# A Fourier-mixing layer and one routed feed-forward token on one core: fewer and longer VectorE operations

## The chip, the core and the metric

One core of a Trainium2 chip runs the whole kernel in one launch. The metric is the device time in microseconds. Each time shown is one execution; the kernel before was run three times, and one more execution was profiled. Where the text says TensorE, VectorE, ScalarE, GpSimd and SP, the profile says PE (and PEld for its weight loads), DVE, ACT, POOL and SP.

## The reference, cut to what matters

With S = 2048 tokens, D = 576 and F = 4608, all float32:

```
h  = x + Re(DFT_seq(DFT_hid(layernorm(x))))   # four matrices given as inputs
z  = layernorm(h)
r  = z @ w_r                                  # one score per token
t  = argmax(r)                                # one token is routed
y  = (silu(z[t] @ w_gate) * (z[t] @ w_up)) @ w_down * sigmoid(r[t])
out = h + z, and y is added to row t
```

## The kernel before

**Data.** x lies in SBUF as X[128, 16, 576], 16 slots of 128 tokens. The sequence matrices (`ct`) are read in blocks of 128 x 9 x 128 float32, 576 KB each. The kernel computes with folded halves of them and of the hidden matrix (`wt`), and it also checks on the chip that the matrices have the symmetry that this folding needs: VectorE forms differences (`off_s`, `off_t`, `off_h`, `off_w`), ScalarE squares and sums them. If the sum is not small, a slower general path runs behind a branch; with these inputs it doesn't. The three weights of the feed-forward part (`wg`, `wu`, `wd`, each 128 x 36 x 576) follow in 27 loads of 1152 KB.

**Stages.** (1) X arrives in nine loads. For each slot, `fold_d` (L454) writes the sum of a row's two mirrored halves and, in a second operation (L466), their difference; `measure` (ScalarE) takes the variance; `from_mean` (L493), `scales` and `diag` (L528) follow for a row group. `X_RUNS` are the five row groups. `diag` writes ident times the slot's 1/sd, a 128 x 128 matrix that TensorE multiplies the folded rows with (`fold`), so that they are scaled on the way. GpSimd does the row groups' small products (`ends`, `totals`, `biases`), whose last line L521 writes the offset column of the folded rows XF. (2) `seq` multiplies XF by the sequence blocks, in two groups of five steps, `hid` by the hidden matrix, and `residual` adds the result to X. Behind it, per slot, ScalarE takes the variance of h and VectorE its product with w_r (`dot_h`, L623). In three batches `scores` (L635 to L644) computes 1/sd, the scores R, and the two factors UP and BB with which ScalarE (`result`, L661) or GpSimd (slots 0 and 8) turns h into the output rows in X; these are stored. (3) `argmax` finds the token, `where`, `row_of_token` (L1039) and `to_all` bring its normalized row to all partitions; `copy_xs` (L1084) writes it to SBUF as xs. (4) The feed-forward part runs in nine blocks of four columns of weights. Products with xs go to VectorE, or to GpSimd with the sums on ScalarE; `gated` (L1225 to L1228) then forms H for four columns with one ScalarE and two VectorE operations, and `down` (L1236) multiplies H by `wd` on TensorE into one row, which `last_of_row` (L1249) adds up and `last_store` writes out.

The dot product subtracts the mean like this: `copy_wr` (ScalarE) spreads w_r over the partitions and keeps its sum; `scores` then computes (h . w_r) - mean(h) sum(w_r) with L639 and multiplies it by 1/sd with L640.

**Order.** Nothing is scheduled by hand. `Plan` takes operations with an engine, a cost in microseconds and what they wait for, and orders each engine's queue by list scheduling; the order is fixed when the program is built. Each queue runs in order, so an operation that waits holds up what is behind it on its engine. SP's queue carries the direct loads and the late stores, GpSimd's queue the mirrored loads (gathers, L301) and the early stores between its arithmetic. A load into a buffer waits for the last reader of what was there. In the feed-forward part there are 16 buffers, so the first 16 loads are issued early and the other eleven each wait for a buffer; `plan_ffn` plans six times and keeps the plan that ends first:

```
for b in range(NJ // TW):
    j = TW * b
    for w in "gu":
        for r in (0, JW):
            products_of(w, j + r)
    gate_and_down(j, j + TW)
    load_to(N_BUF + 3 * (b + 1))
```

`store_if` (L1060) stores slots 4 to 8 and 0 (1440 and 288 KB) under a condition, at one of two places in SP's queue: ahead of the last loads if the token is among those slots, behind them if not.

## Time and profile before

| | us |
|---|---|
| three runs | 199.27, 200.22, 200.1 (median 200.1) |
| the profiled execution | 199.06 |
| its span, first to last instruction | 197.1 |
| busy: PE, DVE, ACT, POOL | 130.2, 166.4, 140.5, 111.8 |
[...]
| moved by DMA | 77.81 MB, mean 395 GB/s |

The busy shares are averages over stages with different limits. An operation's time runs from its start until its result is written, and the next one on the engine can start a little earlier, so sums of busy times come out slightly too large. Idle time of an engine matters only where it delays what ends last.

### The profile page before, as it was taken

What the parts mean: (1) busy time and instruction counts of PE and PEld (TensorE: products, weight loads), DVE (VectorE), ACT (ScalarE), POOL (GpSimd) and SP (SyncE); (2) the same over time, 40 slices, a digit from 0 to 9 for tenths busy, and PEclk for the clock granted to TensorE, in tenths of its full rate; (3) what the DMA queues carried; (4) which work ended last, traced back from release to release, by engine and by line L of the source; (5) the groups of instructions that cost most, each with busy time, mean ns of one, the idle gap of its engine ahead of it and who ended that gap; (6) DMA issues with size and microseconds to landing.
All of it is one profiled execution on the core that took longest, in us unless ns stands there. A gap on an engine that the chain in (4) does not pass through costs nothing. (4 is left out here: it accounts for less than half of the span.)

```text
span 197.1 us, 2789 instructions
## 1 busy us (share of the span) xinstructions
PE 130.2 (66%) x758; PEld 89.5 (45%) x758; DVE 166.4 (84%) x419; ACT 140.5 (71%) x259; POOL 111.8 (57%) x134
## 2 busy tenths in 40 slices
PE   0007889999999999999999986700241317074940
PEld 0004667755667788676866764400121103032330
DVE  4399999989899699995999999999839999987620
ACT  3298865781997879797588599989527999787600
POOL 6588888724447882398830000004556999999700
PEclk9999999999999999999999999985555555567596
DMA  5999999999999999999999999999999999999980
GB/s 183 422 412 413 409 415 406 411 394 326 401 406 396 406 379 410 409 406 415 407 408 416 422 425 419 428 421 409 430 429 417 432 423 425 423 424 421 419 354 24
DMA packets 14491, 77.81 MB, mean 395 GB/s; under 512 B 1855, under 2 KB 1859, under 8 KB 11143
## 3 DMA queue, kind: packets, MB, share of 16 engines
q1 hardware_dynamic: 10461, 56.56, 71.1%
q0 software_dynamic: 4000, 21.03, 26.5%
q8 instruction: 7, 0.11, 0.2%
q14 instruction: 13, 0.11, 0.1%
q10 hardware_dynamic: 10, 0.00, 0.0%
HBM read 72.86 MB, written 6.49 MB: 403 GB/s over the span
## 5 line engine op out<-in xcount | busy, mean ns | idle before, releaser
L368 ACT ACTIVATE Q<-Q 128x2944 bf16<-128x2944 bf16 (+5 forms) x26 | 55.4, 2132 | 15.7 <-DVE Q L380 8.2
L610 PE MATMUL py<-W,Z 128*128 128x289 f32 x180 | 45.3, 409 | 2.5 <-DVE X L619 2.5
L565 PE MATMUL ps<-D,XF 128*128 128x320 f32 (+3 forms) x216 | 44.8, 408 | 0.4 <-DMA D<-in_ct_dram 0.4
L610 PEld LDWEIGHTS py<-W,Z 128*128 128x128 f32 x180 | 33.6, 189 | 13.9 <-issue 2.2
L301 POOL DMA_INDIRECT R<-in_ct_dram,ic x21 | 29.3, 1396 | 18.0 <-DVE Q L375 14.1
L565 PEld LDWEIGHTS ps<-D,XF 128*128 128x128 f32 (+1 forms) x216 | 32.1, 172 | 12.8 <-issue 2.4
L1209 POOL TENSOR_TENSOR D<-D,Z 128x1152 f32<-128x1152 f32 x8 | 20.9, 2640 | 0.0
L667 POOL DMA_DIRECT2D out_dram<-X x1 | 0.6, 606 | 33.5 <-ACT X L661 33.5
L301 POOL DMA_INDIRECT D<-in_ct_dram,ic x11 | 14.8, 1346 | 7.6 <-DMA R<-in_ct_dram,ic 4.6
L498 ACT ACTIVATE junk<-X,XT 128x576 bf16<-128x576 f32 x16 | 12.3, 772 | 7.6 <-DVE W L459 6.4
L1214 ACT ACTIVATE junk<-D 128x576 bf16<-128x576 f32 x20 | 13.7, 683 | 3.2 <-POOL D L1209 1.6
L375 DVE TENSOR_TENSOR Q<-R,D 128x896 bf16<-128x896 f32 x11 | 11.9, 1084 | 3.9 <-DMA D<-in_ct_dram 2.4
L1236 PE MATMUL pd<-XF,H 128*1 128x144 f32 x80 | 5.3, 438 | 14.8 <-DVE H L1228 11.3
L537 PE MATMUL fo<-W,diag 128*128 128x288 f32 (+1 forms) x8 | 3.7, 640 | 16.0 <-DVE diag L528 16.0
L380 DVE TENSOR_TENSOR Q<-R,D 128x1152 bf16<-128x1152 f32 x10 | 13.4, 1348 | 0.0
L630 ACT ACTIVATE junk<-X,TD 128x576 bf16<-128x576 f32 x16 | 12.3, 766 | 1.4 <-DVE X L619 1.3
L661 ACT ACTIVATE X<-X,BB,UP 128x576 f32<-128x576 f32 x14 | 10.8, 854 | 3.1 <-DVE BB L642 3.1
L387 DVE TENSOR_TENSOR Q<-D 128x640 bf16<-128x640 f32 (+3 forms) x20 | 12.8, 694 | 0.0
L623 DVE SCALAR_TENSOR_TENSOR junk<-X,wr 128x576 bf16<-128x576 f32 x16 | 12.1, 755 | 0.3
L375 DVE TENSOR_TENSOR Q<-D 128x896 bf16<-128x896 f32 x11 | 11.8, 1082 | 0.0
L619 DVE SCALAR_TENSOR_TENSOR X<-py,X 128x576 f32<-128x576 f32 x16 | 11.6, 748 | 0.0
L375 DVE TENSOR_TENSOR Q<-R 128x896 bf16<-128x896 f32 x10 | 10.7, 1083 | 0.2 <-DMA R<-in_ct_dram,ic 0.2
(202 smaller groups left out, 257.5 us busy)
## 6 DMA issues: line engine op xcount, KB each, us to landing
D<-in_ct_dram SPq DMA_DIRECT2D x22, 576.0 KB
R<-in_ct_dram SPq DMA_DIRECT2D x10, 576.0 KB
D<-in_wu_dram SPq DMA_DIRECT2D x5, 1152.0 KB
D<-in_wd_dram SPq DMA_DIRECT2D x4, 1152.0 KB
R<-in_wg_dram SPq DMA_DIRECT2D x3, 1152.0 KB
D<-in_wg_dram SPq DMA_DIRECT2D x3, 1152.0 KB
out_dram<-X SPq DMA_DIRECT2D x2, 1440.0 KB
X<-in_x_dram SPq DMA_DIRECT2D x4, 576.0 KB
```

What stands on the lines that cost most here:

```text
L301: pool.indirect_dma_start(tile, None, view, bass.IndirectOffsetOnAxis(ap=rows, axis=0), element_offset=at)
L368: act.activation(t, t, AF.Square, accum_out=DS[0 : t.shape[0], n : n + 1])
L375: dve.tensor_tensor(o, C[j, i, True][:, 0:7, :], C[j, i, False][:, 7:0:-1, :], op=SIGN[i])
L380: dve.tensor_tensor(o, C[NK - j, i, False], C[j, i, False][:, :, ::-1], op=SIGN[i])
L387: dve.tensor_tensor(o[:, :, k::2, :], t[:, :, k::2, 0:HM], t[:, :, k::2, HM:P], op=op)
L498: act.activation(junk[:, 0:D], X[:, k, 0:D], AF.Square, bias=XT[:, n : n + 1], scale=-float(D), accum_out=VX[:, n : n + 1],)
L565: pe.matmul(cm(ZP[g, n][k % 2][p0 : p0 + m], w), XF[:, q, m0 : m0 + m], DT[g, i][:, :, k, 0:HM], start=k in (0, 1), stop=k in (6, 7),)
L610: pe.matmul(YP[GROUPS[g][c]][:, h, 0:w], Z[:, a, c * P : (c + 1) * P], w_block(a)[:, h * HD : h * HD + w], start=(a == 0), stop=(a == 4),)
L623: dve.scalar_tensor_tensor(junk2, X[:, k, 0:D], 1.0, wr, op0=OP.mult, op1=OP.mult, accum_out=TD[:, n, 0:1])
L630: act.activation(junk[:, 0:D], X[:, k, 0:D], AF.Square, bias=TD[:, n, 1:2], scale=-float(D), accum_out=VAR[:, n : n + 1],)
L1209: pool.tensor_tensor(t, t, xs.unsqueeze(1).to_broadcast([P, JW, D]), op=OP.mult)
L1214: act.activation(junk[:, 0:D], WB[w, j][:, r, :], AF.Copy, accum_out=acc[:, j + r : j + r + 1])
```

## The change

- `fold_d` is split: `sum_d` for one slot, `diff_d` for one or two slots that came with one load (six pairs and four singles).
- `from_mean` goes from VectorE to GpSimd, as two operations (the factor D first, then the subtraction).
- 14 `diag` become four `diags`, of 2, 4, 4 and 4 slots, as one product of two operands that repeat (ident over the slots, 1/sd over the columns).
- The one-column copy of `off_w` goes to GpSimd as `off_w0`.
- `copy_wr` subtracts the mean from w_r with a third ScalarE operation, so that `scores` needs only a product; UP and BB are made by `factors` on GpSimd, in three operations, and results and QX wait for those.
- `check_sum` does two comparisons in one operation.
- Blocks 0 and 1, 2 and 3, 4 and 5 of the feed-forward part are gated together; the last three stay single.
- The costs given to the planner change with the operations.

```diff
-        dve.tensor_copy(o[:, 575:576], im[:, 0:1])
+    def off_w0(n, u):
+        ps = W_ROWS[n]
+        pool.tensor_copy(Q[0:ps, u % 2, 3 * D - 1 : 3 * D], W["ABC"[n]][0:ps, 1, 0:1])
...
+    def diff_d(k, m):
+        t, a, b = UF[k][:, 289:D], X[:, k : k + m, 1:HD], X[:, k : k + m, D - 1 : HD : -1]
+        step = UF[k + m - 1].offset - UF[k].offset
+        t = bass.AP(tensor=t.tensor, offset=t.offset, ap=[list(t.ap[0]), [step, m], [1, HD - 1]])
         if k > 8:
             a, b = b, a
-        dve.tensor_tensor(t[:, 289:D], a, b, op=OP.subtract)
+        dve.tensor_tensor(t, a, b, op=OP.subtract)
...
-        pool.tensor_tensor(DX2[:, n0:n1], DX[:, n0:n1], DX[:, n0:n1], op=OP.mult)
+        pool.tensor_scalar(DX2[:, n0:n1], DX[:, n0:n1], float(D), None, op0=OP.mult)
+        pool.tensor_tensor(DX2[:, n0:n1], DX2[:, n0:n1], DX[:, n0:n1], op=OP.mult)
...
-        dve.scalar_tensor_tensor(v, DX2[:, n0:n1], -float(D), v, op0=OP.mult, op1=OP.add)
+        pool.tensor_tensor(v, v, DX2[:, n0:n1], op=OP.subtract)
...
-        dve.tensor_scalar(t, ident, RX[:, n : n + 1], None, op0=OP.mult)
+    def diags(n0, n1, u):
+        m = n1 - n0
+        t = DGT[:, u * P : (u + m) * P].rearrange("p (n c) -> p n c", n=m)
+        dve.tensor_tensor(
+            t, ident.unsqueeze(1).to_broadcast([P, m, P]), RX[:, n0:n1].unsqueeze(2).to_broadcast([P, m, P]),
+            op=OP.mult,
+        )
...
-        dve.scalar_tensor_tensor(r, tot, wsum[:, 1:2], dot, op0=OP.mult, op1=OP.add)
-        dve.tensor_mul(r, r, rs)
-        dve.tensor_scalar(cols(UP, js), cols(RS, js), 1.0, None, op0=OP.add)
-        dve.scalar_tensor_tensor(
-            cols(BB, js), tot, -1.0 / D, cols(RS, js), op0=OP.mult, op1=OP.mult
-        )
+        dve.tensor_mul(r, dot, rs)
+
+    def factors(js):
+        tot, rs = cols(TD, js)[:, :, 1], cols(RS, js)
+        pool.tensor_scalar(cols(UP, js), rs, 1.0, None, op0=OP.add)
+        pool.tensor_tensor(cols(BB, js), tot, rs, op=OP.mult)
+        pool.tensor_scalar(cols(BB, js), cols(BB, js), -1.0 / D, None, op0=OP.mult)
...
+        act.activation(halves_of(wr), YP["wr"][:, :, 0:HD], AF.Identity, bias=wsum[:, 1:2])
+    DG_RUNS = [(0, 2), (2, 6), (6, 10), (10, 14)]
...
         f = add("DVE", 1.5, then(scores, js), v, [n for j in js for n in DOT[j]], push=push)
         SCORES.append(f)
+        f = add("POOL", 0.6, then(factors, js), f, push=push + 10.0)
+        FACTORS.append(f)
...
-    qx = add("DVE", 0.4, from_result, SCORES)
+    qx = add("DVE", 0.4, from_result, FACTORS)
...
-            gate_and_down(j, j + TW)
-            load_to(N_BUF + 3 * (b + 1))
+            if b % 2 or b >= 6:
+                gate_and_down(j0, j + TW)
+                j0 = j + TW
+                load_to(N_BUF + 3 * (b + 1))
```

## Rows read from the trace of the kernel before

**Rows 1.** The page's second part: the DMA line of the span in 40 equal slices. A digit is the mean busy share of the core's 16 DMA engines in tenths.

```profile
DMA  5999999999999999999999999999999999999980
```

**Rows 2.** The stage table: busy time in six stretches of the span. Columns: the stretch and its length in us, busy us (and instructions) of PE, PEld, DVE, ACT and POOL, the granted TensorE clock, the DMA share and the GB/s moved.

```profile
10.00:30.00 20.00, 12.84 (x45) 9.20 (x46) 18.88 (x88) 16.58 (x42) 16.98 (x52) 1.00 1.02 411
30.00:105.00 75.00, 74.34 (x337) 54.35 (x336) 68.88 (x104) 55.81 (x72) 44.97 (x36) 1.00 1.02 399
105.00:130.00 25.00, 19.36 (x78) 14.05 (x76) 24.80 (x55) 20.40 (x35) 0.00 (x0) 1.00 1.01 422
130.00:153.40 23.40, 4.08 (x10) 2.60 (x10) 18.83 (x74) 16.38 (x27) 11.44 (x19) 0.54 1.01 423
153.40:190.50 37.10, 18.79 (x276) 8.93 (x280) 30.62 (x87) 28.58 (x82) 32.34 (x13) 0.60 1.01 422
190.50:197.10 6.60, 0.77 (x28) 0.39 (x16) 0.37 (x1) 0.00 (x0) 0.00 (x0) 0.71 0.21 77
```

**Rows 3.** The instructions in order of time from 186 to 192 us, all engines. Columns: start and length in us, engine, line, operation, output and inputs, count, and in brackets the engine's idle time before it and what ended it.

```profile
188.05 0.16 DVE L1228 TENSOR_TENSOR H<-hs,U 128x4 f32<-128x4 f32 x1
...
190.11 1.16 PE L1236 MATMUL pd<-W,H 128*1 128x144 f32 x32 [0.93 <-SPq L1339]
191.34 0.37 DVE L1249 SCALAR_TENSOR_TENSOR orow<-pd,sg,orow 97x144 f32<-97x144 f32 x1 [3.13 <-PE pd L1236]
```

**Rows 4.** The DMA issues of SP in order of time, over the whole span. Columns as in rows 3. From 153.43 to 170.28 us it issues twelve loads: ten of 1152 KB, and the last as 864 and 288 KB.

```profile
0.86 2.45 SPq L331 DMA_DIRECT2D X<-in_x_dram  x5
...
146.08 0.40 SPq L1060 DMA_DIRECT2D out_dram<-X  x2
153.43 0.35 SPq L1181 DMA_DIRECT2D R<-in_wu_dram  x1
...
158.11 0.33 SPq L1181 DMA_DIRECT2D XF<-in_wg_dram  x1
158.60 0.33 SPq L1181 DMA_DIRECT2D D<-in_wu_dram  x1
...
170.28 0.33 SPq L1183 DMA_DIRECT2D W<-in_wd_dram  x1
173.02 3.13 SPq L1060 DMA_DIRECT2D out_dram<-X  x2
```

**Rows 5.** The DMA issues by tile, with the KB of each. Of the two conditional stores of each size one moves its bytes.

```profile
D<-in_wu_dram SPq DMA_DIRECT2D x5, 1152.0 KB
...
out_dram<-X SPq DMA_DIRECT2D x2, 1440.0 KB
...
out_dram<-X SPq DMA_DIRECT2D x2, 288.0 KB
```

**Rows 6.** The stage table again, columns as in rows 2, for the half microsecond in which the first bytes move and for a stretch of 6 us.

```profile
1.50:2.00 0.50, 0.00 (x0) 0.00 (x0) 0.49 (x2) 0.50 (x1) 0.16 (x1) 1.00 0.69 74
44.00:50.00 6.00, 6.00 (x37) 3.44 (x34) 6.00 (x7) 1.44 (x3) 3.18 (x2) 1.00 1.03 332
```

**Rows 7.** Groups of instructions by line and shape. Columns: line, engine, operation, output and inputs, shapes, count, then busy us and mean ns of one, then the engine's idle time before them and what ended it.

```profile
L375 DVE TENSOR_TENSOR Q<-R,D 128x896 bf16<-128x896 f32 x11 | 11.9, 1084 | 3.9 <-DMA D<-in_ct_dram 2.4 <-ACT Q L368 1.5
...
L528 DVE TENSOR_SCALAR diag<-ident,RX 128x128 f32<-128x128 f32 x14 | 3.2, 281 | 0.1
...
L466 DVE TENSOR_TENSOR D<-X 128x287 f32<-128x287 f32 x7 | 3.2, 451 | 0.0
...
L1227 DVE TENSOR_TENSOR hs<-hs,G 128x4 f32<-128x4 f32 x9 | 1.5, 162 | 3.0 <-ACTq L1339 1.5 <-ACT hs L1225 1.4
...
L485 POOL TENSOR_TENSOR DX<-DX 128x4 f32<-128x4 f32 x3 | 0.8, 261 | 0.2
...
L493 DVE SCALAR_TENSOR_TENSOR VX<-DX,VX 128x4 f32<-128x4 f32 x3 | 0.5, 151 | 0.0
```

**Rows 8.** The instructions in order of time from 139 to 149 us, columns as in rows 3: from the last scores to the copy of the token's row xs.

```profile
139.65 0.22 DVE L639 SCALAR_TENSOR_TENSOR R<-TD,wsum 128x6 f32<-128x6 f32 x1
...
140.24 3.14 ACT L661 ACTIVATE X<-X,BB,UP 128x576 f32<-128x576 f32 x4 [2.40 <-DVE BB L642]
...
143.66 0.17 DVE L1031 SCALAR_TENSOR_TENSOR junk<-QX,hot 128x16 bf16<-128x16 f32 x1
...
144.32 0.96 ACT L1039 ACTIVATE diag<-X,ghp 128x288 f32 x2 [0.93 <-POOL near L1051]
...
148.74 0.65 ACT L1084 ACTIVATE Z<-xsp 128x576 f32<-128x576 f32 x1 [3.46 <-DVE sq L1115]
```

**Rows 9.** The instructions in order of time, columns as in rows 3, at four places: 30 to 33 us, 46 us, 138 us and 162 us, of the engines that the lines name.

```profile
30.20 1.42 DVE L387 TENSOR_TENSOR Q<-D 128x640 bf16<-128x640 f32 x2
30.40 1.27 POOL L513 TENSOR_TENSOR BX<-MX,RX 128x4 f32<-128x4 f32 x1
...
31.93 0.19 POOL L521 TENSOR_TENSOR XF<-V 128x2 f32<-128x2 f32 x1
...
32.87 24.74 PE L565 MATMUL ps<-D,XF 128*128 128x320 f32 x108
...
46.51 1.55 POOL L301 DMA_INDIRECT R<-in_ct_dram,ic  x1 [5.69 <-DVE Q L375]
...
138.26 0.76 DVE L623 SCALAR_TENSOR_TENSOR junk<-X,wr 128x576 bf16<-128x576 f32 x1
...
162.03 2.10 PE L1236 MATMUL pd<-R,H 128*1 128x144 f32 x32 [3.98 <-DVE H L1228]
```

More of the change, by code (lines that the diff above doesn't have):

```diff
@@ L452, with sum_d @@
     UF = {}
-    def fold_d(k):
+    def sum_d(k):
         n = POS[k]
@@ L523 @@
     DG, FO = {}, {}
-    def diag(k, u):
-        n = POS[k]
-        t = DG[k] = DGT[:, u % N_DG * P : (u % N_DG + 1) * P]
-        dve.tensor_scalar(t, ident, RX[:, n : n + 1], None, op0=OP.mult)
+    def diags(n0, n1, u):
[5 more added lines that the diff above has]
+        )
+        for n in range(m):
+            DG[ORDER[n0 + n]] = t[:, n]
     def fold(k):
@@ L733 @@
         e = add("POOL", 0.6, then(ends, a, b), [CAME[k] for k in ks])
-        r = [add("DVE", 0.84, then(fold_d, k), CAME[k]) for k in ks]
+        r = [add("DVE", 0.53, then(sum_d, k), CAME[k]) for k in ks]
+        for k, n in X_LOADS:
+            if k in ks:
+                ns = [(k, n)] if (k, n) != (4, 2) else [(4, 1), (5, 1)]
+                for k, n in ns:
+                    o = add("DVE", 0.15 + 0.3 * n, then(diff_d, k, n), CAME[k])
+                    for q in range(k, k + n):
+                        DIFF[q] = o
         m = [add("ACT", 0.95, then(measure, k), f, push=push) for k, f in zip(ks, r)]
         o = add("POOL", 0.3, then(totals, a, b), e, m)
-        r = add("DVE", 0.2, then(from_mean, a, b), e, m)
+        r = add("POOL", 0.25, then(from_mean, a, b), e, m)
         r = add("ACT", 0.3, then(root, SDX[:, a:b], VX[:, a:b], UNIT), r, push=push)
@@ L769 @@
             at.append(PLACE[n])
+            if k in PAIRS and sl not in DG_OF:
+                r = [n0 for n0, _ in DG_RUNS].index(POS[sl])
+                n0, n1 = DG_RUNS[r]
+                h = r % 2
+                o = add("DVE", 0.15 + 0.133 * (n1 - n0), then(diags, n0, n1, 4 * h), MEAS[sl], dg_users[h], IDENT)
+                dg_users[h] = []
+                for n in range(n0, n1):
+                    DG_OF[ORDER[n]] = o, h
             if k in PAIRS:
-                u, w = dgs.take()
-                dg.append(add("DVE", 0.17, then(diag, sl, u), MEAS[sl], w, IDENT))
-                use.append(u)
+                dg.append(DG_OF[sl][0])
         if k in PAIRS:
@@ L776 @@
             (y0, w0_), (y1, w1_) = of.take(), of.take()
-            f = pe_last = add("PE", 1.95, then(fold, k), dg, w0_, w1_, pe_last)
-            for u in use:
-                dgs.users[u].append(f)
+            f = pe_last = add("PE", 1.95, then(fold, k), dg, DIFF[k], DIFF[NK - k], w0_, w1_, pe_last)
+            dg_users[DG_OF[k][1]].append(f)
             e = [add("ACT", 0.4, then(folded, k, 0), f, BIAS[k]), add("DVE", 0.4, then(folded, k, 1), f)]
@@ L785 @@
             e = last = [
-                add("ACT", 0.55, then(folded, k, 0), BIAS[k]), add("DVE", 0.3, then(folded, k, 1), MEAS[k])
+                add("ACT", 0.55, then(folded, k, 0), BIAS[k]), add("DVE", 0.3, then(folded, k, 1), MEAS[k], DIFF[k])
             ]
@@ L878, in w_check @@
             users[u].append(o)
-            squares(q, 3 * D, o, W_ROWS[n])
-            WS.append(o)
+            f = add("POOL", 0.2, then(off_w0, n, q), WL[n], w)
+            squares(q, 3 * D, [o, f], W_ROWS[n])
+            WS.extend([o, f])
             free.append(u)
@@ L985 @@
             c_first(1, 0, (next(first),))
+        elif step == "c":
+            wc_check()
         else:
```

16 lines of the change are left out of this document (8 added, 8 removed).

## The prediction

> **What bounds the kernel now.** I read the slices of the page first: the DMA line shows 9 from the second slice to the last but two [rows 1]. The stage table says it in numbers: the DMA share is 1.01 to 1.02 in every stage from 10 to 190.5 us and 0.21 in the last 6.6 us [rows 2]. VectorE is close behind, 18.88 of 20 us and 24.80 of 25 us in two stages [rows 2], so it looks like a second bound. Whether it is one depends on how much was queued for the DMA when VectorE was late.
>
> The end: the last matmul group starts at 190.11 us, released by SP's queue, thus by a load; its operand H was ready at 188.05 + 0.16 = 188.2 us [rows 3]. The compute engines are 1.9 us ahead of the data there. What follows the load (1.2 us of TensorE, 0.37 us of VectorE, the store of the row) the change does not touch.
>
> The thinnest point in front of that: SP issues nothing between the store at 146.08 and the load at 153.43 [rows 4]. From 153.4 us to the end 37.1 x 0.422 + 6.6 x 0.077 = 16.2 MB move [rows 2]. Issued in that time are eleven loads of 1152 KB (one of them in two parts) and the late stores of 1440 and 288 KB, which run once: 12.98 + 1.77 = 14.75 MB [rows 4, 5]. So 1.4 MB were still queued at 153.4 us, 3.4 us of transfer. The first load of all, issued at 0.86 us, moves bytes between 1.5 and 2.0 us [rows 4, 6]; I take 1.0 us for that, so the loads could have come 2.4 us later without a gap. Together: the token's row xs may be 1.9 us later (the smaller margin) before the end moves, and may be earlier by any amount without gain. The bytes are the same after the change.
>
> **What the change does, part by part.** *Unit matrices:* 14 operations of 281 ns go; one of 256 and three of 512 elements come. Two-operand rows give 451 ns for 287 elements and 1084 for 896, so 1.04 ns an element on 0.15 us: 0.42 + 3 x 0.68 = 2.5 us against 3.9 us [rows 7]. The old ones overlap by some 0.06 us each, so I take 0.7 us saved. The ends: each joined one as short as an old one (3.9 - 1.1 = 2.8 saved), or repeated operands read at half the rate (0.6 + 1792 x 2.08 ns = 4.3 us, 0.4 to 1.2 lost). The slope of the rows is nearest. *Row differences:* 16 of 0.45 us become ten, six of them with 574 elements, 0.15 + 0.60 = 0.75 us: 7.2 - (6 x 0.75 + 4 x 0.45) = 0.9 us, half of it overlap already. I take 0.4. *Variance fix and one-column cast,* moved: 8 operations of about 0.15 us [rows 7], 1.2 us off VectorE. *Scores:* one operation of 0.22 us [rows 8] and two like the variance fix go, some 0.4 us, three times: 1.2. *Gates:* three of nine pairs go, 3 x 2 x 0.16 = 1.0 us [rows 7]. Sum 4.5 us less VectorE, 3.5 of it before xs exists.
>
> *GpSimd* gets two more small operations for each of five row groups, one for each of three W blocks and three for each of three score batches. Its like takes 0.26 us [rows 7]. 10 x 0.3 = 3 us fall in the stage 10 to 30 us, where it is busy 16.98 of 20 [rows 2], so that is full. The cover: the last offset of the folded rows is there at 32.1 us; the first product over them starts at 32.87 and needs it only near its end (five such steps take 24.74 us, one 4.9) [rows 9]. If TensorE starts 1 to 2 us late all the same, it ends late by as much before 130 us [rows 2], while VectorE has dot products to do until 139.0 [rows 9] and does those first. Counted as nothing. Gathers queued behind it on GpSimd come 3 us later at most, while SP's loads keep the DMA busy; without that cover, 3 us. *ScalarE* gets one more pass over w_r, and ends 1.9 us ahead too.
>
> *The factors' new hop:* UP and BB come from GpSimd after the scores, 3 x 0.3 = 0.9 us behind a hop. Queued behind that: four results on ScalarE from 140.24 to 143.38, two on GpSimd, QX on VectorE. The copy of the row starts at 144.32 and QX is read at 143.66 [rows 8], so 0.9 us for ScalarE and some 2.5 us for QX are cover; late next is the copy of the row, by 0 to 0.2 us, against 0.4 us gained in the same batch and more before. Net, xs comes 1 to 3 us earlier.
>
> *Joined gates:* the down product of blocks 0, 2 and 4 waits for the next block. Behind it waits only its buffer. That of the first down block came free for the load at 158.11; the buffer taken at 158.60 [rows 4] is then free first and takes that load, 0.5 us later, with 1.4 + 2 x 1.18 - 4.7 x 0.42 = 1.8 MB queued, 4.2 us. Nothing. The last three blocks stay single.
>
> The sum against the profiled execution (199.06 us, span 197.1) is 0. It lies 1.04 us under the median of 200.1; carried over, 200.1, and as all that is unsure at the thin points helps, 200.0.
>
> **Rivals.** *A fuller queue, faster.* GpSimd waits 5.69 us for VectorE before it may gather again at 46.51 [rows 9], and around there the rate drops to 332 GB/s for 6 us [rows 6]. If the drop is a thin queue, a VectorE 2 us ahead mends it: 6 x (1 - 332/411) = 1.15 us, 198.9. Against it: the DMA share is 1.03 in the dip, so packets were slow, not missing.
>
> *GpSimd's port, slower.* A product of four columns takes 1.27 us at 30.40, beside VectorE's two-operand differences from 30.20 [rows 9], where its like takes 0.26 [rows 7]. [...] If each of the last three factors takes 1.27 us, the results start 3.8 + 0.2 us late, less 0.9 of cover: xs 3 us late, 1.1 over the margin of 1.9: 201.1, and 201.7 if the full early stage of GpSimd leaves VectorE's gain at nothing too. It decides once xs is 1.9 us late. Against it: VectorE's operations at that point are short, some 0.2 us [rows 8], and so is a wait for one.
>
> *A joined gate holds a load, slower.* If the plan gives the third late load the buffer of the first down block all the same, SP stands until about 164.1, when a down product that starts at 162.03 is through [rows 9], and bytes flow again at 165.1; the 4.2 us queue of 158.1 is empty at 162.3. 2.8 us of gap: 202.8.
>
> *Joined operations no shorter,* as repeated operands are read slower. VectorE then saves 2 to 3 us, and the margin takes that too: 200.0.
>
> **Chances.** Forecast 0.66 and joined operations no shorter 0.03, both no change: 0.69. Fuller queue 0.16, faster. GpSimd's port 0.11 and held load 0.04: 0.15, slower. About 0.5%, 1 us, is what a measurement of this kernel can tell from no change. The range takes in the fuller queue, with 0.2 us more as the 46 us dip is not the only one, and GpSimd's port; it leaves out the held load: 198.7 to 201.7. The forecast's own is 199.3 to 200.8.
>
> **What would show it.** Right: DMA share 1.0 from 10 to 190 us, VectorE 4 to 5 us less busy, joined unit matrices of 512 elements near 0.68 us, GpSimd near full from 10 to 30 us, the copy to xs 1 to 3 us before 148.74 [rows 8], a larger gap than 1.9 us between the last H and the last matmul group, and the end where it was. Wrong: any microsecond between 10 and 190 us with a DMA share under 0.7, the last matmul group released by VectorE, or a dip at 46 us that is gone.

## The result and the profile after

The changed kernel takes 201.22 us (median of 20 executions, 199.5 to 206.48), the kernel before 199.70 beside it (20 executions): ratio 1.0059, interval 1.0036 to 1.0082. It is slower by 0.6%, where no change was forecast. The ratios here leave out executions over 1.5% above a kernel's fastest, so a kernel with many long ones has a median far above its ratio; both are given. The profiled execution took 200.24 us (span 198.5), that of before 199.06 (197.1).

The page's busy line and DMA line [rows 1]:

```profile
PE 130.6 (66%) x758; PEld 91.6 (46%) x758; DVE 163.8 (83%) x379; ACT 141.4 (71%) x257; POOL 125.7 (63%) x156
...
DMA  5999999999899999999999999999999999999993
```

The stage table [rows 2], columns as there:

```profile
10.00:30.00 20.00, 12.56 (x36) 8.90 (x37) 16.04 (x63) 15.45 (x39) 17.44 (x54) 1.00 1.02 412
30.00:60.00 30.00, 30.00 (x131) 20.09 (x130) 27.88 (x41) 20.46 (x25) 16.18 (x24) 1.00 1.00 371
...
90.00:105.00 15.00, 15.00 (x86) 11.60 (x84) 13.14 (x20) 10.68 (x14) 12.05 (x10) 1.00 1.01 390
105.00:130.00 25.00, 20.58 (x82) 14.83 (x80) 24.24 (x46) 20.21 (x34) 0.00 (x0) 1.00 1.01 418
...
191.90:198.50 6.60, 1.98 (x32) 1.05 (x31) 0.37 (x1) 0.00 (x0) 0.00 (x0) 0.50 0.46 184
```

VectorE did get its work off: it is 2.84 us less busy from 10 to 30 us. The DMA line has one 8 where it had a 9, at 50 to 55 us. In the last row there is still a share of 0.46, where before had 0.21 [rows 2]: more bytes are left at the end.

Where the loss begins is read from the instructions in order of time, columns as in rows 3, first after, then before:

```profile
18.53 0.19 POOL L530 TENSOR_TENSOR XF<-V 128x1 f32<-128x1 f32 x1
...
19.43 0.20 POOL L502 TENSOR_TENSOR VX<-VX,DX 128x4 f32<-128x4 f32 x1
...
19.67 0.30 ACT L240 ACTIVATE SDX<-VX,eps 128x4 f32<-128x4 f32 x1 [1.67 <-POOL VX L502]
...
20.00 0.18 DVE L246 RECIPROCAL r0x<-SDX 128x4 f32<-128x4 f32 x1 [1.48 <-ACT SDX L240]
...
20.87 0.69 DVE L537 TENSOR_TENSOR diag<-ident,RX 128x512 f32<-128x512 f32 x1
...
21.62 2.29 PE L551 MATMUL fe<-Z,diag 128*128 128x288 f32 x4 [2.29 <-DVE diag L537]
23.70 3.57 PE L551 MATMUL fo<-Z,diag 128*128 128x287 f32 x12
...
34.84 5.55 PE L579 MATMUL ps<-D,XF 128*128 128x320 f32 x20
...
35.68 0.44 DVE L562 TENSOR_SCALAR XF<-fo 128x287 f32<-128x287 f32 x1
...
52.40 0.80 SPq L357 DMA_DIRECT2D D<-in_ct_dram  x2
```

```profile
17.60 0.15 DVE L493 SCALAR_TENSOR_TENSOR VX<-DX,VX 128x4 f32<-128x4 f32 x1
...
18.32 0.28 ACT L240 ACTIVATE SDX<-VX,eps 128x4 f32<-128x4 f32 x1
...
20.30 1.24 PE L537 MATMUL fe<-Z,diag 128*128 128x288 f32 x4 [0.53 <-DVE diag L528]
21.37 3.07 PE L537 MATMUL fo<-Z,diag 128*128 128x287 f32 x12
...
33.60 0.46 DVE L548 TENSOR_SCALAR XF<-fo 128x287 f32<-128x287 f32 x1 [0.20 <-issue]
...
50.34 0.80 SPq L357 DMA_DIRECT2D D<-in_ct_dram  x2
```

The variance of the second row group, fixed by VectorE at 17.60 before, is now fixed by GpSimd at 19.43. It stands there in program order behind the biases of the first group (L519 to L530, until 18.7) and its own three `ends`. ScalarE's root waits for it 1.67 us, VectorE's reciprocal 1.48, TensorE's folds 2.29. Further on, one delay passes from engine to engine: VectorE's last copy of folded rows (L548 before, L562 after) starts at 35.68 in place of 33.60, its differences follow, and SP issues the load of 50.34 at 52.40, 2.06 us later. From that copy to that load it is 16.74 us before and 16.72 after, so nothing in between takes up any of the delay. At that place the DMA has nothing in store (stage table, after, then before; the third line of after is one microsecond of it):

```profile
50.00:52.50 2.50, 2.50 (x11) 1.79 (x10) 2.50 (x4) 1.38 (x2) 1.89 (x3) 1.00 0.85 301
52.50:55.00 2.50, 2.50 (x11) 1.79 (x10) 1.54 (x3) 2.50 (x3) 0.95 (x1) 1.00 0.91 254
53.00:54.00 1.00, 1.00 (x5) 0.72 (x4) 0.29 (x1) 1.00 (x1) 0.45 (x1) 1.00 0.62 154
```

```profile
50.00:52.50 2.50, 2.50 (x11) 1.79 (x10) 1.55 (x4) 2.50 (x3) 1.07 (x2) 1.00 1.01 401
52.50:55.00 2.50, 2.50 (x10) 1.73 (x10) 2.50 (x3) 2.50 (x3) 1.46 (x1) 1.00 1.02 411
```

Below, the **lag** of a kernel is how far its moved bytes stand behind those of before at the same time: GB/s times length, summed over stretches of 5 us, the difference divided by 0.42 MB/us. After: 0.33 us at 40, 2.06 at 65, 2.25 at 90, 3.23 at 110, 3.24 at 190 us. So about 2 us go from 50 to 65 us, one more from 90 to 110, and nothing behind that.

The end [rows 3]:

```profile
189.72 0.16 DVE L1263 TENSOR_TENSOR H<-hs,U 128x4 f32<-128x4 f32 x1 [1.95 <-ACTq L1377]
...
191.83 2.05 PE L1271 MATMUL pd<-D,H 128*1 128x144 f32 x32 [0.93 <-SPq L1377]
193.93 0.37 DVE L1284 SCALAR_TENSOR_TENSOR orow<-pd,sg,orow 97x144 f32<-97x144 f32 x1 [4.04 <-PE pd L1271]
```

The last matmul group is still released by a load, 1.95 us after its operand H is ready (189.88). It starts 1.72 us later than before. The granted clock over the group is 0.53 of full speed, in before 1.00, and it takes 2.05 us for 1.16. So the last VectorE operation ends 2.6 us later (194.30 for 191.71), but the span is only 1.4 us longer: what is behind that operation takes 4.2 us here and 5.4 in before, and why it is shorter here stays open.

The new operations, by line and shape with columns as in rows 7, cost what was priced: 0.69 us for a joined unit matrix, priced at 0.68, and 0.75 for a joined difference, priced at 0.75.

```profile
L474 DVE TENSOR_TENSOR D<-X 128x574 f32<-128x574 f32 x3 | 2.2, 746 | 0.0
L537 DVE TENSOR_TENSOR diag<-ident,RX 128x512 f32<-128x512 f32 x3 | 2.1, 692 | 0.2
```

### The profile page after: what moved, and what is told of

The parts are those of the page before. It is cut to its first block, busy times and chain, and to the rows that moved or that the text cites. A ratio compares the mean times of both kernels' runs of the same rounds, so it can differ in the third digit from the quotient of the medians.

```text
span 198.5 us, 2771 instructions
## 1 busy us (share of the span) xinstructions
PE 130.6 (66%) x758; PEld 91.6 (46%) x758; DVE 163.8 (83%) x379; ACT 141.4 (71%) x257; POOL 125.7 (63%) x156
## 2 busy tenths in 40 slices
DMA packets 14493, 77.82 MB, mean 392 GB/s; under 512 B 1856, under 2 KB 1860, under 8 KB 11144
## 5 line engine op out<-in xcount | busy, mean ns | idle before, releaser
L301 POOL DMA_INDIRECT R<-in_ct_dram,ic x21 | 33.9, 1613 | 15.8 <-DVE Q L375 11.6
L301 POOL DMA_INDIRECT D<-in_ct_dram,ic x11 | 17.3, 1573 | 3.4 <-issue 3.4
L657 POOL TENSOR_SCALAR UP<-RS 128x6 f32<-128x6 f32 (+1 forms) x3 | 0.7, 245 | 29.3 <-DVE RS L250 29.3
L1244 POOL TENSOR_TENSOR D<-D,Z 128x1152 f32<-128x1152 f32 x7 | 18.3, 2635 | 0.0
L551 PE MATMUL fo<-W,diag 128*128 128x288 f32 (+1 forms) x8 | 4.2, 702 | 15.2 <-POOL VX L502 15.2
L1271 PE MATMUL pd<-D,H 128*1 128x144 f32 x128 | 7.4, 399 | 9.9 <-DVE H L1263 8.7
```

Of the source, the lines that this page charges most:

```text
L301: pool.indirect_dma_start(tile, None, view, bass.IndirectOffsetOnAxis(ap=rows, axis=0), element_offset=at)
L1244: pool.tensor_tensor(t, t, xs.unsqueeze(1).to_broadcast([P, JW, D]), op=OP.mult)
L1271: pe.matmul(T["pd"][at(h), :QD], H[:, j : j + 1], WB["d", j0][:, r, h * QD : (h + 1) * QD], start=(j == 0), stop=(j == NJ - 1),)
```

## The experiments

Each theory names what costs the time. A: `from_mean` stands behind the biases on GpSimd and delays the folds, and with them the load at 50 us. B: the joined gates give buffers back late. C: the factors come late from GpSimd. D: the last matmul group runs at the lower clock. H, added after the first runs: VectorE's differences hold a gather on GpSimd ("held" below: it takes over 5 us), and what needs its rows is late. Two more stand in the expectations: E, GpSimd's load whatever its order; F, the transfers bound the kernel before from end to end. Diffs are cut to their core. In brackets behind a ratio stands its 95% interval.

**e1, the variance fix back on VectorE** (change otherwise whole):

```diff
-        pool.tensor_tensor(v, v, DX2[:, n0:n1], op=OP.subtract)
+        dve.scalar_tensor_tensor(v, DX2[:, n0:n1], -float(D), v, op0=OP.mult, op1=OP.add)
```

> The changed kernel with one part undone: the squared end difference is taken off the variance on VectorE again, as before, and GpSimd has one operation less per group of rows; the loads keep the order of the changed kernel. Theory A (in the changed kernel this operation of the second row group waits in GpSimd's queue behind the first group's biases, runs at 19.43 us, and makes the folds, the stage after them and the loads about 2 us late; the queue of transfers runs dry near 50 us and the time lost there stays lost): the second group's square root starts at 18.0 to 18.5 us in place of 19.67, its unit matrices by 20.0 us in place of 20.87, the L357 load that was issued at 30.68 us is issued by 28.5, the stretch from 30 to 60 us moves about 389 GB/s as before, and the time is 199.0 to 200.0 us (ratio to the kernel before 0.996 to 1.001). Theory B (the joined gates hold buffers back), theory C (factors on GpSimd make the results late) and theory D (the last group of matrix products at the lower clock costs the time): none of them is touched, 201.0 to 201.4 us (ratio about 1.006).

Ratio 1.0002 [0.9956, 1.0049], but the median of its 12 executions is 203.34: four at 199.15 to 201.81, eight at 202.75 to 205.98. The lag at 65 us falls from 2.06 to 1.23. The profiled execution is a long one, 205.63, and shows a second loss (H). The instructions from 62 to 85 us:

```profile
62.49 5.58 POOL L301 DMA_INDIRECT D<-in_wt_dram,iw  x1 [0.30 <-issue]
...
62.63 1.36 DVE L380 TENSOR_TENSOR Q<-R,D 128x1152 bf16<-128x1152 f32 x1
63.90 1.09 DVE L375 TENSOR_TENSOR Q<-R 128x896 bf16<-128x896 f32 x1
...
67.17 1.09 DVE L375 TENSOR_TENSOR Q<-R 128x896 bf16<-128x896 f32 x1
...
76.03 0.76 DVE L422 TENSOR_TENSOR Q<-D,W 128x576 bf16<-128x576 f32 x1 [2.44 <-DMA D<-in_wt_dram,iw]
...
85.04 5.34 PE L623 MATMUL py<-W,Z 128*128 128x289 f32 x14 [2.32 <-DVE X L632]
```

and its stage table, where the second row has the clock at 0.50 behind that wait and the third the rate:

```profile
84.00:86.00 2.00, 0.96 (x3) 0.80 (x4) 2.00 (x5) 1.69 (x1) 2.00 (x1) 0.85 1.00 402
86.00:88.00 2.00, 2.00 (x5) 1.42 (x5) 2.00 (x2) 1.82 (x4) 2.00 (x1) 0.50 1.03 412
90.00:105.00 15.00, 15.00 (x70) 12.19 (x70) 13.42 (x19) 11.12 (x13) 13.39 (x6) 1.00 0.83 288
```

The gather of W's mirrored rows takes 5.58 us, for 1.04 in after (63.25) and 1.03 in before (61.19). Its rows reach VectorE 2.44 us late, the residuals behind them reach TensorE 2.32 us late, and the loads that need the products' buffers come late: the lag is 1.83 at 90 and 6.82 at 110 us.

**e2, before with the variance fix on GpSimd.**

> The kernel before with this part alone: the squared end difference is multiplied by the row length and taken off the variance on GpSimd, two operations of it in place of one and one on VectorE less, every engine's order otherwise as before; in GpSimd's order the subtraction of the second row group stands right behind the first group's biases. Theory A: it runs at about 18.9 to 19.2 us in place of 17.60, the square root of the second group starts about 0.9 us later than 18.32, loads from 28 us on come about 0.9 us later, and the time is 200.3 to 200.7 us (ratio 1.003 to 1.005). Theories B, C and D: 199.6 to 199.9 us (ratio 1.000 to 1.001), since neither gates nor factors are touched and the prediction counted GpSimd's early operations as nothing.

1.0098 [1.0062, 1.0133], median 202.3. The move alone makes before slower, by more than A's 1.003 to 1.005: its first product over folded rows starts at 35.15 for 32.87, and the lag is 2.56 at 65 us. In the profiled execution the gather of 63.47 is held as well, so not all of the time need be A's.

**e3, the change with single gates** (`if b % 2 or b >= 6:` becomes `if True:`).

> The changed kernel with one gate for each two blocks of columns again, as before; the rest is the changed one. Theory A: the gates lie behind transfers, 201.0 to 201.4 us (ratio to the kernel before 1.005 to 1.007), the loads at 30 us and the gap near 50 us as in the changed kernel. Theory B: buffers come free earlier again, 199.7 to 200.2 us (ratio 1.000 to 1.003), and the last load is issued near 170.3 us in place of 173.86.

1.0151 [1.0102, 1.0201], outside the ranges of both theories. Single gates don't bring the time back, so theory B has no support from it; stronger against B is that the lag doesn't grow where the gates lie: 3.23 us at 110 and 3.24 at 190 in after, 4.17 and 4.17 in e3. e3 is later than after already at 65 us (3.44 for 2.06): the load at 50 us comes at 53.86, with a share of 0.42 from 50 to 52.5 us. Why code behind 150 us shifts the work at 20 to 30 us (a joined unit matrix at 31.42, the x12 fold 5.11 us) stays open.

**e4, before with ScalarE late ahead of the second group's root:**

```diff
+        for _ in range(2):
+            act.activation(junk[:, 0:D], X[:, 0, 0:D], AF.Square)
         root(sd, v, eps)
```

> The kernel before with nothing of the change, only a delay at one place: two idle squares on ScalarE (0.78 us and 0.19 us each by their rows, about 1.6 us together as they follow each other) ahead of the square root of the second row group, every engine's order otherwise as before. Theory A: the square root starts at about 19.9 us in place of 18.32, folds, the stage at 33 us and the loads from 28 us on come 1.4 to 2 us later, transfers thin out near 50 us as in the changed kernel, and the time is 200.6 to 201.3 us (ratio 1.004 to 1.008). Theories B, C and D, and the prediction's own step (loads queued ahead cover a delay of this size so early): 199.5 to 199.9 us (ratio 0.999 to 1.001).

1.0088 [1.0053, 1.0123]. A delay put in by itself passes on: the root starts at 19.87, the load at 51.43, and the lag is 1.20. So the chain of A is real whatever causes the delay. The gather of 62.29 is held in the profile, so the whole time isn't A's.

**e5, the second group's `from_mean` ahead of the first group's biases on GpSimd; e6, e1 with the two unpaired rows finished ahead of the last row group; e7, TensorE's wait filled with two repeated matmuls** (one cut of each, in this order):

```diff
+        if a == 2:
+            o0 = add("POOL", 2.0, then(biases, 0, 2), r0, o0, v)
```

```diff
+        o = add("POOL", 2.0, then(biases, a, b), r, o, s[2:])
```

```diff
+        if k == PAIRS[0]:
+            for s in (k, NK - k):
+                pe.matmul(t[:, :w], DG[s], UF[s][:, c : c + w], start=(s == k), stop=(s != k))
```

> The changed kernel with the same instructions on every engine and one difference in GpSimd's order: the subtraction of the second row group stands ahead of the first group's biases in place of behind them. Theory A (the place in the queue costs the time): it runs near 18 us in place of 19.43, the square root of the second group starts by 18.5 us in place of 19.67, TensorE's wait ahead of the second group's folds is under 1.3 us in place of 2.29, loads from 28 us on come 1 us or more earlier than in the changed kernel, and the time is 199.3 to 200.4 us (ratio to the kernel before 0.998 to 1.004). Theory E (it is the number of operations on GpSimd, or what it shares with VectorE, whatever their order): no gain, 201.0 to 201.4 us (ratio 1.005 to 1.007).

> The kernel of the first experiment (the changed one with the subtraction on VectorE) with the order of the kernel before for the two unpaired rows: their root, scales and biases go ahead of the last row group's, which in the first experiment came first and made the stage after the folds start at 34.15 us. Theory A: that stage starts at 32.6 to 33.2 us, the load issued at 51.64 us in the first experiment is issued at 50.0 to 50.7, no more than 0.5 us of transfers is lost against the kernel before by 65 us, and the time is 198.6 to 199.7 us (ratio 0.995 to 1.000). If what is lost near 50 us does not come from the start of that stage: as in the first experiment, ratio 1.000 within its interval, and a lag of about 1.2 us at 65 us.

> The changed kernel with two matrix products of the first fold done a second time, into the same place, so that TensorE's wait of 2.29 us ahead of the second row group is about filled (they take about 2.1 us at the pace of the fold before). Theory A with the pace of TensorE as its second half (of the 2 us by which the stage at 33 us is late, one part is the late square root, and the other that the folds behind the wait run at half their pace: 2.29 us for four passes where the kernel before has 1.24): the second group's folds start as late as in the changed kernel, about 21.6 us, but run at the full pace (1.24 us for four, 3.07 for the next twelve), the stage after them starts at 33.0 to 33.8 us in place of 34.84, and the time is 200.0 to 200.8 us (ratio to the kernel before 1.001 to 1.005). If the late square root alone costs the time: 201.0 to 201.6 us (ratio 1.005 to 1.008), and the stage starts at 34.5 us or later.

e5 1.0179 [1.0129, 1.0229], e6 1.007 [1.0009, 1.0131], e7 1.0031 [0.9969, 1.0093] at a median of 202.99. All three missed, e7 in the start of the stage and not in the ratio. In e5 the folds start at 19.88, and in e7 they take 1.24 and 3.07 us, as in before; yet the first product over folded rows starts at 34.49 and 34.61. The last group of four slots has the same order (in after, biases 26.51 to 28.47, its fix at 28.43 behind them, its unit matrix at 30.01 for 28.49), and the second wait takes back what the first gives. e6 mends both waits (33.12), but its load comes at 51.21 and its lag is 0.79, not 50.7 and 0.5 at most: VectorE, without waiting, reaches its last copy of folded rows at 34.48, in before at 33.60, as more of its own work stands ahead of it. All three have the held gather in the profile, e7 for 6.57 us.

**e8, the factors back on VectorE** (theory C; `pool.` to `dve.` in `factors`).

> The changed kernel with the results' factors on VectorE again (two operations on each group of columns in place of three on GpSimd); all else as in the changed kernel. Theory A: nothing after 110 us costs time, since the transfers' lag stays at 3.2 us from there to 190, so 201.0 to 201.4 us (ratio to the kernel before 1.004 to 1.008). Theory C (the factors on GpSimd make the results or the token's copy late): 199.5 to 200.3 us (ratio 0.999 to 1.003).

1.0226 [1.0177, 1.0275], all six at 203.13 to 205.76, outside the ranges of both theories. Nothing is gained, and as the lag of after is constant behind 110 us, nothing is lost where the factors are made; so C isn't the cause. Here the gather at 64.49 is held for 5.56 us, with a lag of 3.12 already at 65.

**e9, A mended at both places:** as e5, and the last group's subtraction on VectorE; the unpaired rows' biases stay ahead of the last group's.

> The changed kernel with the subtraction mended at both places where it stands behind biases in GpSimd's queue: for the second row group it goes ahead of the first group's biases, as in the experiment that mended this place alone, and for the last row group, whose square root starts at 28.74 us behind another group's biases, it goes to VectorE; the offsets of the unpaired rows keep their place. The other three groups stay on GpSimd. Theory A: the second root starts by 18.0 us, the last by 27.4, the stage after the folds at 32.9 to 33.7 us in place of 34.84, the load of 52.40 us is issued at 50.4 to 51.3, the lag of the transfers at 65 us is at most 1.1 us in place of 2.06, and the time is 199.6 to 200.7 us in executions in which the second of the three gathers for the mirrored hidden matrix takes 1.0 us, and 3 to 4 us more where it takes 5.6, as it did in the executions profiled of most experiments. Theory E (the load on GpSimd, whatever the order): the load at 52.0 us or later, a lag of 2 us.

1.0011 [0.9984, 1.0038], three executions at 199.92 to 200.43 and three at 204.29 to 206.69. The first product starts at 33.45 and the lag is 1.42, but the load comes at 52.00, not at 51.3 or earlier, so A isn't mended whole (e17 shows why). Mending this much of A doesn't take the long executions away.

**e10, e13, e14: H tested.** The six differences beside the gather (62 to 69 us) cover 16 of 128 columns, so that part of the rows is left unsubtracted; e10 has it on e8, e13 on after, e14 on before:

```diff
+        m = 16 if calls[0] in (11, 12, 13, 14) else P
+        dve.tensor_tensor(o[:, :, 0:m], C[j, i, True][:, 0:7, 0:m], C[j, i, False][:, 7:0:-1, 0:m], op=SIGN[i])
```

> The kernel with the factors on VectorE, all of whose six runs took 203 to 206 us, and in whose trace the second gather for the mirrored hidden matrix holds GpSimd for 5.56 us at 64.49, while VectorE runs six differences of the checks without a gap. Here these six are formed over 16 of 128 columns only, some 5.5 us less of VectorE between 63 and 70 us; the rest of their operand keeps older values. Theory H (VectorE's differences hold the gather, the gather then holds the difference that waits for it at 76 us, this a residual, and TensorE): the gather takes 1.2 us or less, TensorE has no wait over 1 us between 78 and 90 us, and the time is 200.6 to 202.3 us (ratio to the kernel before 1.004 to 1.012), what is left being the early lateness. If something else holds it: 5.5 us again and 203 to 205.5 us (ratio 1.017 to 1.026).

> The changed kernel with only the six differences of the checks between 62 and 69 us formed over 16 of 128 columns, as in the experiment that cleared the gather of the kernel with the factors on VectorE; the rest of their operand keeps older values. Theory A alone (the early lateness costs the 0.6%): the early stage is untouched, the lag of the transfers is about 2 us at 65 us, and the time stays at 200.9 to 201.4 us (ratio to the kernel before 1.005 to 1.007). Theory A and H together (the early lateness costs a little, and the rest is what held gathers cost in part of the executions): the same lag of about 2 us, but 199.9 to 200.5 us, no run over 201.5 (ratio 1.000 to 1.004).

> The kernel before with the same six differences over 16 of 128 columns. Theory H: its executions also lose the few that take over 202 us, the others are as they were: 199.2 to 199.9 us (ratio 0.996 to 1.000), none over 201.5. Less of VectorE's work alone gains nothing by theory F (the transfers are the bound from end to end); if it did, 198.5 us or less.

| kernel | all executions, us | median | ratio | lag at 65 / 90 / 110 / 190 us |
|---|---|---|---|---|
| e8 | 203.13 to 205.76 (6) | 205.03 | 1.0226 | 3.12 / 3.55 / 6.01 / 6.04 |
| e10 | 199.84 to 200.31 (6) | 200.17 | 1.0011 [0.9992, 1.003] | 2.37 / 2.61 / 2.64 / 2.65 |
| after | 199.5 to 206.48 (20) | 201.22 | 1.0059 [1.0036, 1.0082] | 2.06 / 2.25 / 3.23 / 3.24 |
| e13 | 198.95 to 200.29, one 204.82 (12) | 199.79 | 1.0001 [0.9975, 1.0028] | 2.21 / 2.36 / 2.42 / 2.50 |
| e14 | 198.79 to 200.07 (12) | 199.58 | 0.999 [0.9965, 1.0014] | 0.14 / 0.29 / 0.33 / 0.37 |

The same gather in e10, beside a narrow difference, and the one that it feeds:

```profile
62.89 0.30 DVE L386 TENSOR_TENSOR Q<-R,D 128x144 bf16<-128x144 f32 x1
...
63.58 0.94 POOL L301 DMA_INDIRECT D<-in_wt_dram,iw  x1 [0.30 <-issue]
...
74.56 0.81 DVE L428 TENSOR_TENSOR Q<-D,W 128x576 bf16<-128x576 f32 x1
```

It takes 0.94 us, VectorE doesn't wait at 74.56, and the long executions are gone from e8's kernel in all six. e13 still has the whole early lag, 2.21 us, and costs nothing measurable; so the narrowing doesn't undo the early lag, but keeps it from growing behind 62 us. It also takes some 5.5 us off VectorE there; that this isn't what helps is shown by e17 below, which subtracts every column and whose lag grows by only 0.53 us from 65 to 190 us. One of e13's twelve still takes 204.82, where none over 201.5 was expected, so these six differences aren't the only source of long executions. In after's own profile the lag grows beside a gather further on:

```profile
63.25 1.04 POOL L301 DMA_INDIRECT D<-in_wt_dram,iw  x1 [0.30 <-issue]
...
78.40 8.92 POOL L301 DMA_INDIRECT R<-in_ct_dram,ic  x1 [0.16 <-DVE Q L425]
...
85.13 1.34 DVE L380 TENSOR_TENSOR Q<-R,D 128x1152 bf16<-128x1152 f32 x1
```

It stands from 78.40 to 87.32, some 0.9 us past the last of six such differences (79.17 to 86.47); the longest gather of e13 there takes 5.51 us. That it adds the third microsecond is argued from the trace, not shown: in e11 the lag grows by 1.33 us from 90 to 110 with no gather longer than 5.51 us there.

How e13 can be 2.5 us late with its bytes and not with its end, shows in the stage table by microsecond, e13, then before:

```profile
190.00:191.00 1.00, 0.37 (x14) 0.35 (x17) 0.00 (x0) 0.00 (x0) 0.00 (x0) 1.00 1.12 465
...
192.00:193.00 1.00, 0.00 (x0) 0.00 (x0) 0.22 (x1) 0.00 (x0) 0.00 (x0) 0.92 0.98 403
193.00:194.00 1.00, 0.00 (x0) 0.00 (x0) 0.00 (x0) 0.00 (x0) 0.00 (x0) 0.50 0.70 273
```

```profile
190.00:191.00 1.00, 0.89 (x32) 0.75 (x32) 0.00 (x0) 0.00 (x0) 0.00 (x0) 1.00 0.87 349
191.00:192.00 1.00, 0.27 (x12) 0.00 (x0) 0.37 (x1) 0.00 (x0) 0.00 (x0) 1.00 0.57 204
192.00:193.00 1.00, 0.00 (x0) 0.00 (x0) 0.00 (x0) 0.00 (x0) 0.00 (x0) 1.00 0.21 82
```

At 190 us before has 0.7 MB left (77.81 less 77.13), e13 1.75 (77.82 less 76.07), about the size of the late stores, 1.77 MB [rows 5]. Its last load lands nearly in time: the last matmul group starts at 190.63, for 190.11 in before and 190.82 in e14, which has a lag of 0.37. So the late stores, which in before move beside the last loads, move behind them here; this is inferred from sizes and times. They are the cover. How far it reaches, all profiled executions show side by side:

| | before | e14 | e16 | e12 | e13 | e9 | e17 | e10 | after | e11 | e7 | e3 |
|---|---|---|---|---|---|---|---|---|---|---|---|---|
| lag at 190 us | 0 | 0.37 | 0.83 | 1.31 | 2.50 | 2.57 | 2.57 | 2.65 | 3.24 | 3.98 | 4.04 | 4.17 |
| last matmul group starts, us | 190.11 | 190.82 | 191.19 | 190.77 | 190.63 | 191.59 | 191.33 | 191.50 | 191.83 | 192.91 | 193.48 | 192.81 |
| time, us | 199.06 | 199.66 | 200.21 | 199.61 | 199.59 | 200.43 | 200.12 | 200.24 | 200.24 | 201.57 | 201.31 | 201.45 |

| | e8 | e4 | e5 | e6 | e1 | e2 |
|---|---|---|---|---|---|---|
| lag at 190 us | 6.04 | 6.36 | 6.64 | 6.76 | 8.93 | 10.54 |
| last matmul group starts, us | 194.61 | 195.56 | 195.37 | 195.21 | 197.60 | 200.08 |
| time, us | 203.13 | 204.16 | 203.34 | 203.77 | 205.63 | 207.98 |

Up to 2.65 us of lag the times lie between 199.06 and 200.43 without order; from there to 10.54 us they rise from 200.24 to 207.98, 7.7 us for 7.9. The last matmul group says it more closely than the time, in which what follows it also varies. From 1.31 us of lag on, it starts later than in before by the lag less 0.6 to 2.0 us. That is the cover, and e13 is its best case: four kernels with lags of 2.50 to 2.65 us start this group 0.5 to 1.5 us later. How the 16 engines share stores and loads stays open.

**e11, e12: the checks of VectorE at 32 to 38 us** (four differences over 8 of 64 columns) made shorter, on after and on before.

> The changed kernel with four differences of the check (those at 36.05 to 38.7 us, behind the last copy of the folded rows on VectorE) over 8 of 64 columns only, about 1.9 us less of VectorE there; the rest of their operand is zero. The unit matrices, the folds and the stage after them stay as late as in the changed kernel. Theory A with VectorE as its last link (the late folds hold VectorE's last copies, these the checks behind them, and the loads from 40 us on wait for the checks to have read their buffers): the loads of 42.09 and 52.40 us are issued about 1.9 us earlier, the lag of the transfers at 65 us is at most 0.7 us in place of 2.06, and the time is 199.4 to 200.5 us where the second gather for the mirrored hidden matrix is not held. Rival (the loads wait for TensorE's late stage): both loads and the lag as in the changed kernel, 201.0 to 201.5 us.

> The kernel before with the same four differences over 8 of 64 columns, so that its own loads of 40.03 and 50.34 us are issued about 1.9 us earlier; nothing of the change is in it. Theory F (the kernel before moves all that the transfers can move; the low rate at 45 to 50 us is slow packets): no more than 0.5 us of transfers ahead of the kernel before at 65 us, and 199.2 to 200.2 us (ratio 0.997 to 1.001). Rival, the fuller queue of the prediction (the low rate is a thin queue, and a VectorE that is 2 us ahead mends it): 1 us or more ahead at 65 us, and 198.2 to 198.9 us (ratio 0.991 to 0.995).

e11 1.0032 [0.999, 1.0075], e12 0.9999 [0.9969, 1.0029]. Both missed in the size of the shift: the load at 50 us comes only 0.3 and 0.5 us earlier, in e12 because VectorE then waits 1.35 us for ScalarE's squares. e12 has its bytes 0.36 us ahead at 65 us and gains nothing measurable; that speaks against the fuller-queue rival, but at half a microsecond, not at the 2 us that it asks for. In its profile the gather at 60.69 is held too, for 6.57 us, and the lag grows from 0.13 us at 90 to 1.31 at 190; its time is 199.61 us. So a held gather isn't by itself the loss.

How far the lag then grows goes with a second gather, at 78 to 86 us. From 90 to 110 us it grows by 2.5 to 5.0 us where both were held (e1, e2, e4, e5, e6, e8), by 1.2 where only the first was (e7, e12), by 0.03 to 1.33 where only the second was (after, e3, e9, e10, e11, e13), and by less than 0.1 where neither was (before, e14, e16, e17). No run changes the second by itself, so this is read side by side, not tried.

**e16, e17: a pause for the gather, nothing left out.** A one-element VectorE copy waits for GpSimd to be through with the gather; e16 on before, e17 on e9:

```diff
+            pool.memset(gone, 0.0)
+            dve.tensor_copy(seen, gone)
```

> The kernel before, complete, with a pause on VectorE ahead of the run of six differences: a one-element copy that waits until GpSimd is through with the second gather for the mirrored hidden matrix. Theory H: the gather takes 0.9 to 1.1 us in every execution, VectorE stands 1.5 to 2 us, which its wait of 1.80 us at 69.07 us gives back, and the time is 199.3 to 200.2 us, none over 202 (ratio 0.997 to 1.002). Rival: the pause makes the loads behind these differences late, the transfers thin out near 70 us, 200.5 to 201.5 us (ratio 1.004 to 1.009).

> The change, complete and mended: the subtraction at both places as in the experiment that mended both, and the pause on VectorE of the experiment beside this. Theories A and H: a lag of the transfers of 1 to 1.6 us at 65 us, the gather at 0.9 to 1.1 us, 199.4 to 200.4 us, none over 202 (ratio to the kernel before 0.998 to 1.003), so level with the kernel before and no better, since the transfers bound both. If it beats the kernel before by over 0.3%, theory F is wrong.

e16 1.0021 [0.9994, 1.0047], all 12 at 199.49 to 200.65; e17 1.0057 [1.0028, 1.0087], all 12 at 199.49 to 202.07. The gather takes 0.93 and 0.94 us, with every column subtracted, and of e17's twelve executions none is over 203 us, where three of six were in e9; so H doesn't rest on the narrowing. e16 can't show it, as the kernel before has one in 35 over 203 beside it. The expectation for e17 missed: its first product starts at 33.35, yet its load at 50 us comes at 52.48 and its lag is 2.04 at 65 us. The trace says where that comes from:

```profile
34.15 0.64 POOL L535 TENSOR_TENSOR BE<-BX 128x2 f32<-128x2 f32 x1
...
34.83 0.50 ACT L565 ACTIVATE XF<-fe,BE 128x288 f32<-128x288 f32 x1 [3.74 <-POOL BE L535]
...
35.75 0.46 DVE L567 TENSOR_SCALAR XF<-fo 128x287 f32<-128x287 f32 x1 [1.01 <-ACT XF L565]
```

GpSimd is through with the last group's offsets (BE) at 34.79 us, 31.97 in before. ScalarE waits 3.74 us for them, and VectorE's last copy of folded rows 1.01 us for ScalarE; from that copy to the load it is 16.73 us again. Four of GpSimd's last products (32.20 to 34.79) run beside VectorE's differences (31.99 to 34.74) and take 0.49 to 0.78 us each; in e6, where they come ahead of the differences, the like take 0.20 to 0.34. So GpSimd makes the early stage late by two ways, and moving the fix mends one of them. The lag of 2.57 us at the end starts the last matmul group 1.22 us later, which is in size e17's 0.6%. No version beats the kernel before.

What the load at 50 us is worth in lag, over ten of the kernels:

| | e12 | before | e6 | e4 | e1 | e9 | after | e7 | e8 | e3 |
|---|---|---|---|---|---|---|---|---|---|---|
| load issued, us | 49.84 | 50.34 | 51.21 | 51.43 | 51.64 | 52.00 | 52.40 | 52.73 | 53.62 | 53.86 |
| lag at 65 us | -0.36 | 0 | 0.79 | 1.20 | 1.23 | 1.42 | 2.06 | 2.25 | 3.12 | 3.44 |

From 49.84 to 53.86 us, 4.02 us of issue, the lag rises by 3.80: about one for one, with no margin on the late side of before.

## Why the prediction was wrong

**What held.** The DMA stays the bound, and the last group waits for a load. The joined operations cost their slope. At the joined gates no bytes are lost (lag 3.23 us at 110 and 3.24 at 190). GpSimd is near full early, 17.44 of 20 us. VectorE is less busy, but by 2.6 us (166.4 to 163.8) in place of 4 to 5. The time lies in the range, 201.22 in 198.7 to 201.7, on its slower side, and not for the reasons that set the range.

**The step that failed** is the one on GpSimd's early operations, "Counted as nothing". Its size was right: TensorE "starts 1 to 2 us late", 34.84 for 32.87. Its cover was wrong, twice. "SP's loads keep the DMA busy": at 50 us SP's loads themselves wait for buffers that VectorE empties behind the folds, and a late copy is a late load, 2.06 us late in after. And "the thinnest point in front of that" was placed at 153 us with 2.4 us of margin, while there is a thinner one at 50 us with none; the share of 1.01 there in before meant just full, not a queue. The prediction's own sign of being wrong came there: a share of 0.62 from 53 to 54 us. The last offset's cover was read for TensorE alone, while in e17 ScalarE waits 3.74 us for it and VectorE 1.01 behind that. The term was priced for GpSimd's own busy time (10 operations), but not for the order on it: one result of 0.20 us stood behind 3 us of biases that nobody was yet waiting for.

**What made it a small loss** is a cover that the prediction didn't see, the late stores, worth 0.6 to 2.0 us. e13 has the early lag and no measurable loss. So the early lag of 2.06 us uses up most or all of the cover, and what the lag gains behind 62 us comes through: in after's profile one microsecond more, and where gathers are held far more (in e1 from 1.23 us at 65 to 8.93 at 190). That the early lag and the later growth add up to the 0.6% is argued from the lags; taking away the growth (e13, 1.0001) or part of the early lag (e9, 1.0011, over three of its six executions) each leaves no measurable loss, but e17, with no held gather and 2.04 us of early lag, has 0.6%, which e13 with 2.21 us hasn't. What decides between 1.03 and 5.58 us for the gather is open: in all thirteen profiles with these differences whole and without the pause, VectorE starts the next one 0.12 to 0.14 us behind the gather's start. Whether the change makes it more frequent isn't shown either. In after 5 of 20 executions are over 203 us, in before none of 20 beside it, but 6 of 97 over all comparisons (up to 206.22). The clock isn't what sets them apart: its mean is 0.847 to 0.869 in these five, 0.846 to 0.877 in after's others.

**The rivals.** GpSimd's port came nearest, though no run shows what its name says. Its sign is right, and GpSimd's work does take longer beside VectorE's differences (in e17 0.49 to 0.78 us, for 0.20 to 0.34 in e6), but not at its place: it put the delay on the last three factors, while the rows have it on the last group's products at 32 to 35 us and on gathers at 62 and 78 us, which GpSimd also issues. That the median lies in its 201.1 to 201.7 is luck, as its sum went by xs being over its margin, which cost nothing. No run shows its term of 1.27 us for each of the last three factors: in after they took 0.24, 0.19 and 0.25 us (142.63 to 143.39). The gather took 5.58 us in e1 beside whole differences and 0.94 in e10 beside narrow ones, but 1.03 to 1.04 us in five profiles beside whole ones; so a whole difference beside it isn't enough to hold it, and what else it takes stays open. The factors did cost more than priced: from R to the results 2.11 us (141.31 to 143.42) for 0.59 [rows 8], so 1.5 for 0.9, since GpSimd issued a scatter of rows first (141.50, 0.95 us). With the dot products late as well, xs came at 151.07, 2.3 us later, not 1 to 3 earlier. That is over the margin of 1.9 us and still cost nothing, as the bytes were 3.2 us late too. A fuller queue has no support: with 2.6 us less of VectorE after isn't faster, and e12 gained nothing from 0.36 us of bytes ahead. D is real in part: the last group takes 2.05 us in after and 1.16 in e13, 0.9 us at the end of after's profiled execution.

## What to carry over

Before a small operation moves to another engine, look at what stands ahead of it in that engine's order, and follow its reader until a DMA issue: a delay of a 0.2 us operation came out as 2 us of missing transfers 30 us later. A DMA share of 1.0 says that the engines are busy, not that anything is queued (before has 1.01 from 50 to 52.5 us; with one load there 2.06 us later, after has 0.62 from 53 to 54); margin has to be shown stretch by stretch, as by issuing one load a little later there. And a lag in the middle need not arrive at the end (e13: 2.21 us at 65, the last matmul group 0.52 us late): follow it to the last load before crediting a time to it.

## What was not expected of the hardware

- The same gather at the same place in VectorE's run of differences took 1.03 or 1.04 us in five profiles and 5.56 to 6.57 us in eight.
- In several kernels folds behind a TensorE wait (of 2.29 us in after) ran at about half pace with the granted clock recorded as 1.00: x4 2.29 us for 1.24, x12 3.57 to 5.11 for 3.07. With TensorE kept at work (e7) they took 1.24 and 3.07, but the wait isn't shown to be the cause: e10 has the same wait of 2.29 us and 1.24 and 3.07, and e2 has 2.29 and 4.26 behind a wait of 0.56. Behind the 2.32 us wait of e1 the recorded clock did fall, to 0.50.
- Of a lag of 2.50 to 2.65 us in moved bytes, only 0.5 to 1.5 us arrived at the last matmul group; that stores that nobody waits for moved last is inferred from sizes and times.
